# Balancing the gate's sums: one operation folded, six expert items between column sums, a lower rate beside the recurrence

## The chip, the core and the metric

The kernel runs on one core of a Trainium2 chip. The metric is the device time of one launch in microseconds (us). The engines are TensorE (PE; PEld is its loading of weights), VectorE (DVE), ScalarE (ACT), GpSimd (POOL) and SyncE (SP), which issues most transfers.

## What is computed

Three layers, one behind the other. The first is a delta-rule recurrence over 768 steps for 4 x 8 heads of 48; its output is 3072 tokens of 384 channels. The second is a mixture of eight experts in which every token goes through every expert, weighted by a gate matrix P of 3072 x 8 that is balanced by eight rounds of row and column normalization:

```python
    logits = x @ w_gate
    logits = logits - logits.max()
    P = np.exp(logits)
    for _ in range(8):
        P /= P.sum(1, keepdims=True) + 1e-09
        P /= P.sum(0, keepdims=True) + 1e-09
        P *= N / E
    ...
    for e in range(E):
        h = np.maximum(x @ w1[e], 0.0)
        out += P[:, e:e + 1] * (h @ w2[e])
```

The third layer is a feed-forward block with a sigmoid gate (384 to 2048 to 384). Everything is float32; the large products run as three matmuls of split halves each (lines 480 to 482).

## The kernel before

**Recurrence and expert 0 (to about 507 us).** The recurrence is cut into 24 chain steps `u` with four products each: `ks` (L354), `up` (L365), `sp` (L376), `y` (L389). Each needs DVE or ACT between one and the next: L356 makes `r` for `up`, L382 the new state. Every four chain steps share a preparation `prep(g)`: masked products (L181), then the solving of triangular systems on DVE, thirty pairs of L276 and L280, then a transpose (L298) and small products on PE (L307, L316). The steps of `prep` are spread over slots by the table `PIECES`.

To keep PE busy, the work of expert 0, which needs the tokens but not the gate, is cut into 480 **items** of three matmuls each: `g1` (first layer, tile `ph`, 256 columns, three items for one h) and `g2` (second layer, tile `po`, 384 columns). Each h costs one ACT (L626) and one DVE instruction (L627). `slot(t)` puts a number of items into each of the chain's slots: `rate * ITEMS[t % 16]`, where `rate = RATE * 8 / sum(ITEMS)`. So RATE is the mean number of items of two slots; it is 9.6. The first items come at slot LAG.

**Balancing the gate (507 to about 543 us).** After the last logits (transposed by L612 and copied to P by L613) the generator `sinkhorn()` runs while the left-over items go out: every SKN-th item of the loop at L890 advances it by one step. Its steps are: the maximum (L660; L663, a transpose; L665; L668, the matmul that spreads it), subtracting it (L670, L671), the exponential on ACT (L672, with a table load), and eight iterations. One iteration: row sums (L677 to L680, DVE), the sum over a partition's rows (L681), the matmul with ones that sums over partitions (L684, tile `psk`), and then the column scale (L685 to L688). Between two steps stand SKN items, here 5. The same loop issues the loads of the main loop's tokens (`load_x`) at every third item and steps the first main weights (`weights1(0)`, on ACT and POOL) at every third.

**Main loop (from about 543 us).** Seven experts and the third layer, in units of 15 products (`c`) and 12 groups (`po`), with PE as the bound. Tile order, buffers and the program order of all engines are written out by hand (`manual_schedule`).

What sets the order around the change is therefore the code's own order: each engine runs its instructions in the order in which the code emits them, and waits only for data and buffers.

Of the kernel before, what the change touches and what calls it, by code (L numbers as in the profile page):

```python
# [14 lines left out]
ALU = mybir.AluOpType  # L15
# [9 lines left out]
NE = 8  # L25
NT = 3072
# [6 lines left out]


LAG = 10
RATE = 9.6
BURST = 6
SKN = 5


class Attention:
# [400 lines left out]
def kernel(  # L442
# [4 lines left out]
    nc = tc.nc  # L447
# [207 lines left out]
    def sinkhorn():  # L655
        def col(ps_shape):
            return sm["ps"].tile(ps_shape, F32, tag=sm["tag"], name="psk")

        mx = pp.tile([128, 1], F32, name="mx")
        nc.vector.tensor_reduce(out=mx, in_=P.rearrange("p u e -> p (u e)"), op=ALU.max, axis=AX.X)  # L660
        yield
        pt = col([1, 128])
        nc.tensor.transpose(pt, mx, ident)  # L663
        m1 = pp.tile([1, 1], F32, name="m1")
        nc.vector.tensor_reduce(out=m1, in_=pt, op=ALU.max, axis=AX.X)  # L665
        yield
        pb = col([128, 1])
        nc.tensor.matmul(pb, ones[0:1, :], m1, start=True, stop=True)  # L668
        nm = pp.tile([128, 1], F32, name="nm")
        nc.vector.tensor_scalar(out=nm, in0=pb, scalar1=-1.0, scalar2=None, op0=ALU.mult)  # L670
        nc.vector.tensor_scalar(out=P, in0=P, scalar1=nm, scalar2=None, op0=ALU.add)  # L671
        nc.scalar.activation(out=P, in_=P, func=ACTF.Exp)  # L672
        rs = pp.tile([128, NU], F32, name="rs")
        c1 = pp.tile([128, NE], F32, name="c1")
        c2 = pp.tile([128, NE], F32, name="c2")
        for _ in range(8):
            nc.vector.reduce_sum(out=rs, in_=P, axis=AX.X)  # L677
            nc.vector.tensor_scalar(out=rs, in0=rs, scalar1=1e-9, scalar2=None, op0=ALU.add)
            nc.vector.reciprocal(out=rs, in_=rs)
            nc.vector.tensor_tensor(out=P, in0=P, in1=rs.unsqueeze(2).to_broadcast([128, NU, NE]), op=ALU.mult)  # L680
            nc.vector.reduce_sum(out=c1, in_=P.rearrange("p u e -> p e u"), axis=AX.X)  # L681
            yield
            pc = col([128, NE])
            nc.tensor.matmul(pc, ones, c1, start=True, stop=True)  # L684
            nc.vector.tensor_scalar(out=c2, in0=pc, scalar1=1e-9, scalar2=None, op0=ALU.add)  # L685
            nc.vector.reciprocal(out=c2, in_=c2)
            nc.vector.tensor_scalar(out=c2, in0=c2, scalar1=float(NT // NE), scalar2=None, op0=ALU.mult)
            nc.vector.tensor_tensor(out=P, in0=P, in1=c2.unsqueeze(1).to_broadcast([128, NU, NE]), op=ALU.mult)  # L688

    ex = []  # L690
# [1 line left out]
    def expert_item():  # L692
        while ex:
            if next(ex[0], None) is not None:
                return True
            ex.pop(0)
        return False
# [7 lines left out]

    rate = RATE * 8 / sum(ITEMS)
    done, due = 0, 0.0
# [60 lines left out]
    pc = ctx.enter_context(tc.tile_pool(name="pc", bufs=1, space=PSUM, **tw))  # L768
# [117 lines left out]
    loads = [r for r, *_ in SCHEME]  # L886
    w0 = weights1(0)
    sk = sinkhorn()
    sm["ps"], sm["tag"] = pc, "c"
    for i in range(60 * 8 - done):  # L890
        expert_item()
        if i % SKN == 0:
            next(sk, None)
# [274 lines left out]
```

## Time and profile before

| | us |
|---|---|
| three timed runs | 2259.91, 2262.90, 2262.99 (median 2262.9) |
| profiled execution: span from first to last instruction | 2254.7 |
| PE busy in it | 2151.8 (95%) |
| DVE busy | 1525.3 (68%) |
| POOL busy | 1113.1 (49%) |
| ACT busy | 1059.9 (47%) |

The profiled execution's own time is not listed apart from its span; the median of the timed runs is 8.2 us above the span. The shares are averages over stages with different limits. In the first 60 us PE is mostly idle and the recurrence starts alone. From there to 507 us recurrence and expert 0 run side by side, and 507 to 543 us is the balancing of the gate. The rest, three quarters of the time, is the main loop.

### The profile page before, as it was taken

Reading aid. Unit: us, or ns where it says so; the run is one execution under the profiler, and the core shown is the slowest. Engines: PE = TensorE matmul, PEld = TensorE weight load, DVE = VectorE, ACT = ScalarE, POOL = GpSimd, SP = SyncE. Lnnn points to the kernel's source line nnn. Section 1 sums busy time; section 2 is a strip of 40 time slices with the busy share of each in tenths; the row PEclk is TensorE's granted clock in tenths of the full one; section 3 lists DMA queues with packets and bytes.
Section 4 is the critical chain, followed back from the end, with each engine's and each line's share of the span. In section 5 each row is a group of like instructions: output and inputs, shape, how many; then the busy total and the mean of one; then the engine's idle time right before and its main releaser. Section 6 shows DMA issues by size and latency. Waiting matters only on the chain.

```text
span 2254.7 us, 40816 instructions
## 1 busy us (share of the span) xinstructions
PE 2151.8 (95%) x15663; PEld 1935.9 (86%) x15663; DVE 1525.3 (68%) x2770; ACT 1059.9 (47%) x2125; POOL 1113.1 (49%) x1293
## 2 busy tenths in 40 slices
PE   4499999998999999999999999999999999999999
PEld 4388888896989899999998888888989998888888
DVE  6666866626776776666666777777775556676675
ACT  2334343544444444444445444454544446565554
POOL 5521132214677766666552556566665434662333
PEclk7599999999999999999999999999999999999999
DMA  5223333338435343333447655555564465567231
GB/s 116 67 82 83 89 98 101 92 110 312 145 114 182 123 167 134 125 132 114 153 183 252 189 170 183 171 194 175 187 198 143 130 242 170 164 186 240 92 119 50
DMA packets 229155, 336.75 MB, mean 149 GB/s; under 512 B 15648, under 2 KB 192416, under 8 KB 224800
## 3 DMA queue, kind: packets, MB, share of 16 engines
q1 hardware_dynamic: 228240, 333.26, 46.0%
q8 instruction: 123, 2.02, 0.4%
q10 hardware_dynamic: 720, 0.89, 0.1%
q14 instruction: 72, 0.59, 0.1%
HBM read 204.58 MB, written 129.50 MB: 148 GB/s over the span
## 4 chain that ended last, share of the span: by engine, by line
PE 76%; DVE 12%; POOL 3%; DMA 3%; issue 2%; ACT 2%; SPq 1%; POOLq 0%; ACTq 0%; DVEq 0%
PE po L480 13%; PE po L482 13%; PE po L481 13%; PE c L480 10%; PE c L481 9%; PE c L482 9%; DVE ln L280 3%; DVE lt L276 3%; PE pg L181 2%; PE ph L480 1%; DMA w1r<-in_w_dram 1%; POOL w1c L477 1%; PE ph L481 1%; PE ph L482 1%; PE y L389 1%
## 5 line engine op out<-in xcount | busy, mean ns | idle before, releaser
L481 PE MATMUL po<-w2c,h 128*128 128x384 f32 x1728 | 586.8, 340 | 0.0
L482 PE MATMUL po<-w2c,h 128*128 128x384 f32 x1728 | 585.2, 339 | 0.9 <-DVE h L981 0.7
L480 PE MATMUL po<-w2c,h 128*128 128x384 f32 x1728 | 578.4, 335 | 1.0 <-ACT h L979 1.0
L1036 POOL TENSOR_TENSOR acc<-acc,ye 128x384 f32<-128x384 f32 x252 | 264.1, 1048 | 387.1 <-ACT ye L1035 374.0
L480 PE MATMUL c<-xt,w1c 128*128 128x512 f32 x1080 | 430.6, 399 | 11.5 <-DVE h L972 5.5
L482 PE MATMUL c<-xt,w1c 128*128 128x512 f32 x1080 | 429.3, 397 | 1.7 <-POOL w1c L477 1.7
L481 PE MATMUL c<-xt,w1c 128*128 128x512 f32 x1080 | 428.3, 397 | 0.0
L1013 DVE TENSOR_TENSOR o<-o,c 128x512 f32<-128x512 f32 x288 | 197.2, 685 | 251.2 <-PE c L482 232.6
L480 PEld LDWEIGHTS po<-w2c,h 128*128 128x128 f32 x1728 | 324.6, 188 | 40.8 <-ACT h L979 1.6
L481 PEld LDWEIGHTS po<-w2c,h 128*128 128x128 f32 x1728 | 323.5, 187 | 40.0
L1038 DVE SCALAR_TENSOR_TENSOR acc<-po,P,acc 128x384 f32<-128x384 f32 x420 | 257.9, 614 | 147.1 <-PE po L482 143.5
L482 PEld LDWEIGHTS po<-w2c,h 128*128 128x128 f32 x1728 | 324.7, 188 | 1.5 <-DVE h L981 1.5
L1035 ACT ACTIVATE ye<-po,P 128x384 f32<-128x384 f32 x252 | 146.3, 581 | 361.8 <-PE po L482 352.7
L482 PEld LDWEIGHTS c<-xt,w1c 128*128 128x128 f32 x1080 | 202.6, 188 | 47.1 <-POOL w1c L477 2.7
L480 PEld LDWEIGHTS c<-xt,w1c 128*128 128x128 f32 x1080 | 203.0, 188 | 42.7 <-DVE h L972 18.1
L481 PEld LDWEIGHTS c<-xt,w1c 128*128 128x128 f32 x1080 | 203.2, 188 | 9.0
L1006 ACT COPY o<-c 128x512 f32<-128x512 f32 x288 | 163.8, 590 | 54.2 <-PE c L482 53.0
L970 ACT ACTIVATE h<-c 128x512 fp32r<-128x512 f32 x168 | 96.8, 598 | 181.2 <-DVE c L1013 173.4
L1048 POOL TENSOR_TENSOR acc<-acc,ye 128x384 f32<-128x384 f32 x84 | 92.8, 1104 | 166.2 <-ACT ye L1047 156.4
L477 POOL TENSOR_TENSOR w2c<-w2r,w2c 128x384 fp32r<-128x384 f32 x140 | 147.4, 1053 | 45.6 <-ACT w2c L476 45.5
L1013 DVE TENSOR_TENSOR f<-o,c 128x512 f32<-128x512 f32 x216 | 148.9, 689 | 12.4 <-PE c L482 3.4
L970 ACT ACTIVATE h<-f 128x512 fp32r<-128x512 f32 x168 | 100.1, 596 | 79.6 <-DVE f L1013 76.0
(174 smaller groups left out, 3524.5 us busy)
## 6 DMA issues: line engine op xcount, KB each, us to landing
w1c<-wd SPq DMA_DIRECT2D x210, 384.0 KB, 4.5
wd<-w1c SPq DMA_DIRECT2D x28, 1920.0 KB, 7.0
xs<-bo SPq DMA_DIRECT2D x184, 128.0 KB, 2.2
xt<-xs SPq DMA_DIRECT2D x46, 512.0 KB, 5.8
w2r<-in_w_dram SPq DMA_DIRECT2D x55, 384.0 KB, 5.8
wd<-wo SPq DMA_DIRECT2D x56, 256.0 KB, 3.0
w1r<-in_w_dram SPq DMA_DIRECT2D x28, 384.0 KB, 7.6
x<-in_kq_dram SPq DMA_DIRECT2D x24, 384.0 KB, 6.6
```

The source lines that it names most:

```text
L276: nc.vector.tensor_tensor(out=t3, in0=ln[:, jj + 1:32, jj:jj + 1].to_broadcast([128, nr, jj]), in1=ln[:, jj:jj + 1, 0:jj].to_broadcast([12 ...
L477: eng.tensor_tensor(out=dst_lo, in0=src, in1=dst_hi.bitcast(F32), op=ALU.subtract)
L480: nc.tensor.matmul(ps, lhs[0], rhs[0], start=start, stop=False, **kw)
L481: nc.tensor.matmul(ps, lhs[0], rhs[1], start=False, stop=False, **kw)
L482: nc.tensor.matmul(ps, lhs[1], rhs[0], start=False, stop=stop, **kw)
L970: nc.scalar.activation(out=h[:, 0], in_=src, func=ACTF.Relu)
L1006: nc.scalar.copy(out=o, in_=ps)
L1013: nc.vector.tensor_tensor(out=d, in0=o, in1=ps, op=ALU.add if how == "add" else ALU.subtract)
L1035: nc.scalar.mul(ye, ps, P[:, u, e:e + 1])
L1036: nc.gpsimd.tensor_tensor(out=a, in0=a, in1=ye, op=ALU.add)
L1038: nc.vector.scalar_tensor_tensor(out=a, in0=ps, scalar=P[:, u, e:e + 1], in1=a, op0=ALU.mult, op1=ALU.add)
L1048: nc.gpsimd.tensor_tensor(out=a, in0=a, in1=ye, op=ALU.add)
```

## The change

Three constants and one operation. RATE goes from 9.6 to 9.2, so each slot of the recurrence gets 4% fewer items, and more are left for the loop behind it. SKN goes from 5 to 6. In the column scale, the factor NE / NT is multiplied in by the second operation of the instruction that adds 1e-9, ahead of the reciprocal, instead of NT / NE by an instruction of its own behind it.

```diff
-RATE = 9.6
+RATE = 9.2
 BURST = 6
-SKN = 5
+SKN = 6
...
             pc = col([128, NE])
             nc.tensor.matmul(pc, ones, c1, start=True, stop=True)
-            nc.vector.tensor_scalar(out=c2, in0=pc, scalar1=1e-9, scalar2=None, op0=ALU.add)
+            nc.vector.tensor_scalar(out=c2, in0=pc, scalar1=1e-9, scalar2=float(NE) / NT, op0=ALU.add, op1=ALU.mult)
             nc.vector.reciprocal(out=c2, in_=c2)
-            nc.vector.tensor_scalar(out=c2, in0=c2, scalar1=float(NT // NE), scalar2=None, op0=ALU.mult)
             nc.vector.tensor_tensor(out=P, in0=P, in1=c2.unsqueeze(1).to_broadcast([128, NU, NE]), op=ALU.mult)
```

Behind this place, line numbers of the changed kernel are one lower.

On PE, in the recurrence (rows with + are the changed kernel's, with - the kernel's before; `ph` and `po` are items of expert 0, `w1s` and `w2s` its weights):

```order
 L482 MATMUL po<-w2s_196,h 128x384
+L354 MATMUL ks<-S,x_126 64x48 x16
 L480 MATMUL ph<-xb,w1s_191 128x256
 L481 MATMUL ph<-xb,w1s_191 128x256
 L482 MATMUL ph<-xb,w1s_191 128x256
-L354 MATMUL ks<-S,x_126 64x48 x16
```

The chain's product comes one item earlier; such differences add up to 17 items at the last logits.

On DVE, one iteration of the balancing before (`psk` is the sum over partitions, `c_6935` the column scale):

```order
L685 TENSOR_SCALAR c_6935<-psk 128x8
L686 RECIPROCAL c_6935<-c_6935 128x8
L687 TENSOR_SCALAR c_6935<-c_6935 128x8
L688 TENSOR_TENSOR P<-P,c_6935 128x192
L677 TENSOR_REDUCE rs<-P 128x24
L678 TENSOR_SCALAR rs<-rs 128x24
L679 RECIPROCAL rs<-rs 128x24
L680 TENSOR_TENSOR P<-P,rs 128x192
L681 TENSOR_REDUCE c_6934<-P 128x8
L627 SCALAR_TENSOR_TENSOR h<-ph,h 128x256
```

And one after, with the same names:

```order
L685 TENSOR_SCALAR c_6877<-psk 128x8
L686 RECIPROCAL c_6877<-c_6877 128x8
L687 TENSOR_TENSOR P<-P,c_6877 128x192
L677 TENSOR_REDUCE rs<-P 128x24
L678 TENSOR_SCALAR rs<-rs 128x24
L679 RECIPROCAL rs<-rs 128x24
L680 TENSOR_TENSOR P<-P,rs 128x192
L681 TENSOR_REDUCE c_6876<-P 128x8
L627 SCALAR_TENSOR_TENSOR h<-ph,h 128x256
```

The scalar instruction between reciprocal and product is gone, and the order of the others is kept.

On ACT, around the exponential before (`ye` is a result of expert 0 that is written out, `lg` the logits, `w1c` the first main weights):

```order
L606 COPY lg<-pl 8x256
L626 ACTIVATE h<-ph 128x256 x2
L642 COPY ye<-po 128x384
L643 DMA yd<-ye 128x384
L642 COPY ye<-po 128x384
L643 DMA yd<-ye 128x384
L672 ACT_TABLE_LOAD
L672 ACTIVATE P<-P 128x192
L626 ACTIVATE h<-ph 128x256 x3
L476 CAST w1c<-w1r 128x256
```

And after:

```order
L606 COPY lg<-pl 8x256
L626 ACTIVATE h<-ph 128x256 x3
L672 ACT_TABLE_LOAD
L672 ACTIVATE P<-P 128x192
L626 ACTIVATE h<-ph 128x256
L476 CAST w1c<-w1r 128x256
L626 ACTIVATE h<-ph 128x256
L476 CAST w1c<-w1r 128x128
L642 COPY ye<-po 128x384
L643 DMA yd<-ye 128x384
```

The two results `ye` that stood ahead of the table load stand behind the exponential.

## Rows read from the trace of the kernel before

**Rows 1.** Windows, 180 to 507 us: length, PE, PEld, DVE, ACT, POOL busy, PEclk, DMA.

```profile
180.00:209.00 29.00, 27.02 (x377) 24.59 (x375) 27.63 (x81) 9.97 (x25) 3.76 (x4) 1.00 0.41 111
209.00:252.00 43.00, 43.00 (x772) 37.15 (x768) 22.22 (x49) 19.01 (x36) 9.04 (x7) 1.00 0.29 76
252.00:283.00 31.00, 28.89 (x415) 25.90 (x416) 29.10 (x88) 11.40 (x28) 4.09 (x4) 1.00 0.40 103
...
322.00:358.00 36.00, 33.12 (x421) 30.45 (x418) 33.51 (x89) 13.59 (x33) 10.37 (x14) 0.91 0.44 111
...
400.00:433.00 33.00, 30.49 (x429) 28.03 (x427) 30.87 (x80) 13.36 (x32) 6.25 (x11) 1.00 0.35 104
433.00:507.00 74.00, 74.00 (x1143) 68.16 (x1135) 18.71 (x39) 34.07 (x76) 15.88 (x27) 1.00 0.31 93
```

**Rows 2.** Timeline of PE in the recurrence: start, duration, instruction, [idle before <- releaser].

```profile
337.41 1.94 PE L365 MATMUL up<-r,tt 64*64 64x48 f32 x32 [2.31 <-DVE r L356]
...
414.79 1.13 PE L365 MATMUL up<-r,tt 64*64 64x48 f32 x32 [1.49 <-DVE r L356]
```

**Rows 3.** Timeline of PE from the last logits to the main loop.

```profile
507.11 0.28 PE L612 MATMUL pt<-ident,lg 8*128 8x8 f32 x2
...
512.90 0.38 PE L668 MATMUL psk<-m,ones 1*128 1x1 f32 x2
...
517.85 0.39 PE L684 MATMUL psk<-c,ones 128*128 128x8 f32 x2 [2.59 <-DVE c L681]
...
539.27 0.39 PE L684 MATMUL psk<-c,ones 128*128 128x8 f32 x2 [0.74 <-DVE c L681]
...
542.63 0.39 PE L684 MATMUL psk<-c,ones 128*128 128x8 f32 x2 [0.23 <-DVE c L681]
542.88 0.48 PE L480 MATMUL c<-xt,w1c 128*128 128x512 f32 x1
```

**Rows 4.** Timeline of DVE in one iteration of the balancing.

```profile
536.79 0.17 DVE L687 TENSOR_SCALAR c<-c 128x8 f32<-128x8 f32 x1
537.00 0.36 DVE L688 TENSOR_TENSOR P<-P,c 128x192 f32<-128x192 f32 x1
...
539.13 0.42 DVE L627 SCALAR_TENSOR_TENSOR h<-ph,h 128x256 fp32r<-128x256 f32 x1
```

**Rows 5.** Timelines of DVE and ACT around the exponential.

```profile
513.51 0.62 DVE L671 TENSOR_SCALAR P<-P,nm 128x192 f32<-128x192 f32 x1
...
514.28 1.28 ACT L672 ACT_TABLE_LOAD   x1 [0.39 <-ACT ye L642]
515.58 0.36 ACT L672 ACTIVATE P<-P 128x192 f32<-128x192 f32 x1
```

**Rows 6.** Timeline of PE: two matmuls of a first-layer and of a second-layer item.

```profile
537.13 0.28 PE L480 MATMUL ph<-xb,w1s 128*128 128x256 f32 x1
537.25 0.28 PE L481 MATMUL ph<-xb,w1s 128*128 128x256 f32 x1
...
541.37 0.33 PE L481 MATMUL po<-w2s,h 128*128 128x384 f32 x1
541.54 0.33 PE L482 MATMUL po<-w2s,h 128*128 128x384 f32 x1
```

**Rows 7.** Timelines of DVE and POOL at two long DVE instructions.

```profile
526.00 0.71 DVE L687 TENSOR_SCALAR c<-c 128x8 f32<-128x8 f32 x1
...
524.86 1.82 POOL L477 TENSOR_TENSOR w1c<-w1v,w1c 128x768 fp32r<-128x768 f32 x1 [2.06 <-ACT w1c L476]
...
543.87 0.86 DVE L688 TENSOR_TENSOR P<-P,c 128x192 f32<-128x192 f32 x1
...
543.76 0.75 POOL L834 TENSOR_TENSOR w1v<-w1r 128x256 f32<-128x256 f32 x1
```

**Rows 8.** Windows behind two waits of PE, columns as in rows 1 (PEclk third from last).

```profile
337.40:343.90 6.50, 6.49 (x49) 6.41 (x50) 5.58 (x15) 2.19 (x5) 0.00 (x0) 0.50 0.02 6
414.80:418.00 3.20, 3.20 (x47) 3.10 (x47) 2.96 (x9) 1.43 (x3) 0.00 (x0) 1.00 0.00 0
```

## The prediction

> **What bounds the kernel now.** I read the windows of busy time first, to see which engine limits which stretch, then the timeline around the column sums, where most of TensorE's (PE's) idle time after the start lies. Behind 545 us PE is nearly always busy and the change leaves the order of work there as it is, so the question is how long PE takes to reach that point. PE's work in front of it is the same before and after: 480 expert items and the recurrence. Only PE's idle time can change.
>
> Beside the recurrence two engines take turns. In four stretches (180 to 209, 252 to 283, 322 to 358, 400 to 433 us) VectorE (DVE) solves the triangular systems: it is busy for 27.6 of 29.0 us in the first, in some 80 instructions, and the gaps are the hand-overs between them. PE stands idle for 1.98, 2.11, 2.88 and 2.51 us in these, 9.5 us in all, though it is nearly full too. Between them PE has no gap: 43.00 of 43.00 us, and at the end 74.00 of 74.00 [rows 1]. Where PE does wait, it is for what DVE makes late, as the product with r in the third and the fourth solve, 2.31 and 1.49 us [rows 2].
>
> Behind the recurrence come the alternating sums (the tail): from the transpose of the last logits, 507.11 us, to the first product of the main loop, 542.88, it is 35.77 us [rows 3]. The DVE chain sets the pace: the eighth sum's matmul starts 3.36 us behind the seventh's, although PE has only five items to do in between. An item is three matmuls with a start-to-start of 0.12 us (first layer) or 0.17 us (second) [rows 6], so 0.36 or 0.51 us. In 480 items first and second stand 24 to 16, which makes 0.42 us on average. Five items are some 2.1 us in a period of 3.36. And in front of the first of the eight sums PE waits 2.59 us [rows 3]. The 51 items of this tail are worth 27 x 0.36 + 24 x 0.51 = 22.0 us of its 35.77.
>
> **What moves.** Counting items in the program's order: at the transpose of the last logits 429 items lie behind PE before, 412 after; 17 items go from beside the recurrence into the tail, which has 68 instead of 51. Two of the 17 are gone by the product with r of chain step 5, 15 leave between there and the end. Between two sums there are six items instead of five, and behind the eighth sum seven (one first, six second) instead of none. The eight iterations lose one DVE instruction each.
>
> **Recurrence.** If PE were the bound everywhere, 17 x 0.42 = 7.1 us would go. In the four solves it isn't: they are 29 + 31 + 36 + 33 = 129 of the 357 us from 150 to 507, 36% [rows 1]. I put 36% of the 15 items, 5.4, into them. There an item is worth only its share of DVE: one instruction of 0.42 us (L627 [rows 4]) in five items, 5.4 x 0.42 / 5 = 0.45 us. The other 9.6 items are worth 9.6 x 0.42 = 4.0 us. The two early ones I give nothing (in full they would be 0.8). Sum: the recurrence ends **4.5 us** earlier. The bounds: 7.1 us from above; from below, if only the two windows in which PE never waited [rows 1] give all of it back, 117 / 357 x 15 x 0.42 = 2.1 us. The cover that hides an item's removal in a solve is DVE's own queue; if that cover is thinner than I think, the gain goes up, not down.
>
> **Tail, up to the first sum.** From the last logits (T0) to the matmul that spreads the maximum (L668) it is now 5.79 us for 11 items [rows 3], which by their kinds are 3 x 0.36 + 8 x 0.51 = 5.2, so 0.6 us of small matmuls. After it is 13 items, 8 first and 5 second: 5.4 + 0.6 = 6.0. From L668 to the first sum it is 4.95 us now [rows 3]. Of this, the exponential waits: its input was ready at 513.51 + 0.62 = 514.13, but the table load began only at 514.28 and the exponential at 515.58 [rows 5], because two evictions of an expert's result stood ahead of the load on ScalarE (ACT). In the new order these two stand behind the exponential, and what stands ahead is an eviction of h, done by about L668. The load then runs beside L670 and L671 and the exponential can start near 514.17, 1.4 us earlier by this clock. That gives 4.95 - 1.4 = 3.55, and the first sum at T0 + 9.6 us instead of 10.74. PE's six items there (2.6 us) are hidden.
>
> A page speaks against this. The Trainium skill, "ScalarE: Activation LUTs", section "What ACT_TABLE_LOAD costs", counts a switch at about 2.66 us, 1.28 for the load and the rest for a drain. The trace doesn't agree here: the exponential starts at 515.58, 0.02 us behind the end of a load of 1.28 us [rows 5]. By the page's price the exponential would come 1.4 us later than I take it and the result would be 2260.7 us.
>
> **Tail, the eight sums.** Removed are eight L687, 0.17 us and 0.04 us to the next instruction [rows 4], so the period of 3.36 becomes 3.15 us; six items are 2.6 us and the sum's matmul 0.25 [rows 3], so DVE still sets it, with PE close behind. Seven periods: 22.05 us. With six items one period gets two L627, and in another the h comes out of the last item before the sum, so its L627 stands late in DVE's queue ahead of the next sum's first instruction; I take 0.4 us for each, 0.8 together. Between nothing and these 0.8 I choose the upper value, since the order shows both.
>
> Some L687 took longer: 0.71 us at 526.00, ending with GpSimd's (POOL's) subtraction of 524.86 + 1.82. It reads as a wait of 0.54 us for POOL. The removal would give this back if the next instruction were free of it. But L688, with both inputs in SBUF, took 0.86 us instead of 0.36 at 543.87, beside POOL's work of 543.76 [rows 4, 7]. So the wait passes on to the next instruction, and I count it as kept: 0.5 us, half of the 0.54 + 0.50 seen, from zero to 1.0, because other instructions meet POOL's now. The Trainium skill, "SBUF — State Buffer", section "Who interferes with whom", says the same against this part of the change: a DVE instruction with two SBUF inputs also blocks against a GpSimd instruction that reads SBUF. Without that rule the forecast would be 0.5 us lower.
>
> Behind the eighth sum: 0.25 us for its matmul and 0.36 + 6 x 0.51 = 3.4 of items, with 0.1 for the hand-over: 3.75 us, where it was 0.25. Sum of the tail: 9.6 + 22.05 + 0.8 + 0.5 + 3.75 = 36.7 us, **0.9 us longer** than now, with 17 items more in it. The lower bound is 9.6 + 22.05 + 3.75 = 35.4 (0.4 shorter); the upper has the exponential no earlier (1.4) and all of the POOL waits (another 0.5): 38.6, 2.8 longer.
>
> Folding the scale into the addition itself costs nothing: L685 stays one instruction on the same eight columns. The transfers for the main loop are issued at the same item numbers of a longer tail, so they land earlier against its start; I count nothing for it.
>
> **Sum.** 4.5 - 0.9 = 3.6 us less. The profiled span of 2254.7 becomes 2251.1. The median of the three runs lies 8.2 us above that span, and I leave this distance: **2259.3 us**. The bounds together: gain of 7.1 + 0.4 = 7.5 (2255.4) to 2.1 - 2.8 = -0.7 (2263.6).
>
> **Rivals.**
> (a) PE is the bound beside the recurrence after all: DVE's lateness in the solves comes from PE's own lateness, and the full 7.1 us come off. Then 2262.9 - 7.1 + 0.9 = 2256.7. For it: PE is 92 to 93% busy even in the solves. Against: DVE is busy for 93 to 95% of each of them [rows 1], and PE waits for its results there [rows 2].
> (b) Slower: PE's waits grow until the clock falls. Behind the wait of 2.31 us the granted clock was 0.50, the lower of its two levels (1.2 and 2.4 GHz), for 337.40 to 343.90; behind that of 1.49 us it stayed at 1.00 [rows 2, 8]. Fewer items leave about 0.57 us more waiting in each solve (5.4 x 0.42 / 4). That would bring the 1.49 to 2.1, and if it and its like in the two other solves reached 2.3, each would cost half of 6.5 us: 3 x 3.25 = 9.75, to 2269.0. It decides from 2.3 us on in one wait; against it, the additions fall 0.2 us short at the worst place and more elsewhere.
> (c) The change moves work but frees nothing: only the windows without a wait give time back (2.1) and the tail takes its upper bound (2.8 longer): 2263.6.
>
> **How the numbers follow.** The forecast has 50% (2257 to 2261.5), (a) 28%, (c) 14%, (b) 8%. A measurement of this kernel can tell about 0.2%, 4.5 us, from no change. Faster than that means below 2258.4: all of (a) and some 8 of the forecast's 50, 36%. Slower means above 2267.4: (b), 8%. The rest, 56%, lies within. The range from 2256.0 to 2264.0 takes in the forecast, (a) and (c), and leaves out (b) and the outer ends.
>
> **What would show it.** The time of the last logits' transpose: 502.6 us if the recurrence is as I say, near 500 for (a). From there to the main loop's first product: 36.7. In front of the first sum PE should wait under 1 us instead of 2.59, and the half clock behind it should be gone. Period of the sums: near 3.2. The half clock near 337 us should neither vanish nor have companions. I am wrong if the main loop, from its first product to the end, changes by more than 2 us: then something is moved that I did not see.

## The result: slower, and outside the range

The changed kernel takes 2288.2 us (median of six runs, 2271.9 to 2295.6) against 2263.0 for the kernel before in the same comparison: a ratio of 1.0095, 95% interval 1.007 to 1.012. Forecast were 2259.3 us and a range of 2256.0 to 2264.0. The profiled execution is one of the quicker ones: 2274.9 us, span 2273.2. Of its 18.5 us more than the profile before, 9.8 lie in front of the last logits, 5.3 in the tail and 3.4 in the main loop.

TensorE (PE) in the tail after, to be read against [rows 3] (start, duration, instruction, [idle before <- releaser]):

```profile
516.90 0.28 PE L612 MATMUL pt<-ident,lg 8*128 8x8 f32 x2
...
522.94 0.38 PE L668 MATMUL psk<-m,ones 1*128 1x1 f32 x2
...
526.77 0.39 PE L684 MATMUL psk<-c,ones 128*128 128x8 f32 x2 [0.61 <-DVE c L681]
...
533.12 0.39 PE L684 MATMUL psk<-c,ones 128*128 128x8 f32 x2
...
539.07 0.60 PE L684 MATMUL psk<-c,ones 128*128 128x8 f32 x2 [2.09 <-DVE c L681]
...
544.46 0.43 PE L684 MATMUL psk<-c,ones 128*128 128x8 f32 x2
...
550.84 0.39 PE L684 MATMUL psk<-c,ones 128*128 128x8 f32 x2 [0.21 <-DVE c L681]
```

The last logits (T0) come at 516.90 instead of 507.11; 502.6 was forecast. From there to the main loop's first product (557.96) it is 41.06 us instead of 35.77. The first sum is where it should be, 9.87 us behind T0, with 0.61 us of waiting. But the fourth and the fifth sum come 5.95 and 5.39 us behind the one before them, where 3.15 was forecast.

PE's waits beside the recurrence, to be read against [rows 2]. `issue` means that PE waited for nothing that the profile names:

```profile
296.59 0.65 PE L181 MATMUL pg<-x 48*64 48x128 f32 x6 [0.30 <-issue]
...
340.02 1.27 PE L365 MATMUL up<-r,tt 64*64 64x48 f32 x19 [2.98 <-DVE r L356]
...
376.00 0.87 PE L181 MATMUL pg<-x 48*64 48x128 f32 x12 [1.07 <-issue]
...
411.43 0.42 PE L480 MATMUL ph<-xb,w1s 128*128 128x256 f32 x1 [2.75 <-DVE h L627]
...
485.78 1.52 PE L365 MATMUL up<-r,tt 64*64 64x48 f32 x24 [5.36 <-ACT h L626]
```

The wait of 2.31 us has become 2.98, and there are new ones: two with no visible cause, one of 2.75, and one of 5.36 us, the largest between 150 us and T0. Windows with the granted clock (third from last), to be read against [rows 1, 8]:

```profile
209.00:252.00 43.00, 42.75 (x770) 37.17 (x771) 22.17 (x51) 19.00 (x36) 9.42 (x8) 1.00 0.29 76
...
336.00:347.00 11.00, 7.76 (x64) 7.19 (x65) 9.77 (x26) 2.19 (x5) 0.19 (x1) 0.53 0.06 17
...
433.00:517.00 84.00, 77.75 (x1185) 72.31 (x1183) 22.89 (x47) 37.07 (x82) 19.26 (x34) 0.96 0.29 86
...
483.00:491.00 8.00, 5.22 (x47) 5.01 (x47) 1.78 (x4) 3.64 (x9) 5.37 (x10) 0.57 0.00 0
```

The last stretch in front of T0, in which PE had no gap before (74.00 of 74.00 us), has 6.25 us of idle time now, and near 340 and 487 us the clock is at its lower level. The two stretches between solves that carried the forecast's gain give nothing back: from `up` of step 7 to that of step 9 it is 43.8 us instead of 44.0, and from `up` of step 19 to T0 83.0 instead of 77.3.

### The profile page after: what moved, and what is told of

It is laid out like the page before. It is cut to its first block, busy times and chain, and to the rows that moved or that the text cites. A ratio compares the mean times of both kernels' runs of the same rounds, so it can differ in the third digit from the quotient of the medians.

```text
span 2273.2 us, 40799 instructions
## 1 busy us (share of the span) xinstructions
PE 2159.6 (95%) x15663; PEld 1945.3 (86%) x15663; DVE 1526.8 (67%) x2762; ACT 1059.6 (47%) x2125; POOL 1113.2 (49%) x1293
## 3 DMA queue, kind: packets, MB, share of 16 engines
q8 instruction: 123, 2.02, 0.3%
## 4 chain that ended last, share of the span: by engine, by line
PE 76%; DVE 12%; POOL 3%; DMA 3%; ACT 2%; issue 2%; SPq 1%; POOLq 0%; ACTq 0%; DVEq 0%
PE po L482 13%; PE po L480 13%; PE po L481 13%; PE c L480 10%; PE c L481 9%; PE c L482 9%; DVE ln L280 3%; DVE lt L276 3%; PE pg L181 2%; PE ph L480 1%; DMA w1r<-in_w_dram 1%; POOL w1c L477 1%; PE ph L481 1%; PE ph L482 1%; PE up L365 1%
## 5 line engine op out<-in xcount | busy, mean ns | idle before, releaser
L1034 ACT ACTIVATE ye<-po,P 128x384 f32<-128x384 f32 x252 | 146.3, 581 | 359.4 <-PE po L482 346.3
```

The lines of the kernel that those rows point to most:

```text
L1034: nc.scalar.mul(ye, ps, P[:, u, e:e + 1])
```

## The experiments

All 18 experiments in one table, below the two kernels; what each is for follows. Ratio: to the kernel before in the same comparison. T0 and the stalls (`issue`, over 0.2 us) are from the profiled execution, and "half clock" is the time at 0.50 between 150 us and T0, worked out from windows of 1 us.

| kernel | median | ratio, 95% | T0 | half clock | stalls |
|---|---|---|---|---|---|
| before | 2263.0 | | 507.1 | 6.8 | none |
| after | 2288.2 | 1.0095 (1.007 to 1.012) | 516.9 | 20.4 | 0.30, 1.07 |
| e1 RATE alone | 2294.4 | 1.0138 (1.0113 to 1.0162) | 534.6 | 54.6 | 2.05, 2.23 |
| e2 all but RATE | 2265.7 | 1.0008 (0.9993 to 1.0023) | 508.2 | 6.8 | none |
| e3 no lump | 2282.7 | 1.0086 (1.0052 to 1.0121) | 531.5 | 54.6 | 2.64, 2.04 |
| e4 writes on ScalarE's queue | 2301.3 | 1.0163 (1.0131 to 1.0195) | 545.5 | 75.0 | 1.81, 1.91 |
| e5 after, one block | 2288.1 | 1.0107 (1.0075 to 1.0138) | 528.0 | 40.9 | 2.20, 0.25 |
| e6 after, two blocks | 2294.3 | 1.0125 (1.009 to 1.0159) | 543.3 | 68.1 | 1.92, 1.68 |
| e7 before, one block | 2266.8 | 1.0012 (0.9997 to 1.0027) | 512.6 | 13.6 | none |
| e8 no lump, one block | 2281.0 | 1.0073 (1.0045 to 1.0102) | 519.2 | 30.7 | 1.92 |
| e9 after, half a block | 2274.0 | 1.0050 (1.0028 to 1.0072) | 517.9 | 27.2 | none |
| e10 before, half a block | 2266.8 | 1.0020 (0.9998 to 1.0041) | 517.2 | 20.5 | 1.15 |
| e11 no lump, half a block | 2268.1 | 1.0022 (1.0007 to 1.0037) | 516.5 | 23.8 | none |
| e12 x later | 2274.3 | 1.0051 (1.0032 to 1.0069) | 517.5 | 27.2 | none |
| e13 as e11, RATE 8.8 | 2265.8 | 1.0017 (1.0005 to 1.0029) | 506.0 | 20.4 | none |
| e14 before, RATE 10.0 | 2307.0 | 1.0196 (1.0173 to 1.0218) | 557.0 | 64.8 | none |
| e15 fold alone | 2262.0 | 0.9996 (0.9985 to 1.0008) | 511.0 | 13.6 | none |
| e16 before, fillers | 2265.9 | 1.0012 (0.9998 to 1.0026) | 510.6 | 6.8 | none |
| e17 e11, fillers | 2267.9 | 1.0018 (1.0004 to 1.0033) | 512.9 | 10.2 | 1.41 |
| e18 e13, fillers | 2268.7 | 1.0027 (1.0011 to 1.0042) | 502.6 | 6.8 | none |

### Which part of the change: e1 to e4

My first theory came from the two programs' order, read once more. Tokens arrive in batches of 40 items, one every two chain steps, and the loop at L737 (`while u % 2 == 1 and len(ex) > 1`) must finish a batch before the next is split, since `xb` has two buffers. RATE 9.6 just keeps up. RATE 9.2 falls behind, and the rest is done in one piece, a **lump**, between `up` and the transposes of x: 3, 7, 10 and 13 items at chain steps 17, 19, 21 and 23. I had counted items at T0, 17 fewer, and taken them as evenly spread.

The kernel before with the new rate alone (e1):

```diff
-RATE = 9.6
+RATE = 9.2
```

> The kernel before with one number changed: RATE 9.2 in place of 9.6. In its order 3, 7, 10 and 13 expert items stand in one piece ahead of the transposes of x at chain steps 17, 19, 21 and 23. If these lumps make the kernel slower (theory L): last logits after 512 us, median 2272 to 2295 us. If the fold or the sixth item between two sums does it (theory F): last logits near 503, median 2258 to 2264.

The changed kernel with the old rate (e2):

```diff
-RATE = 9.2
+RATE = 9.6
```

> The changed kernel with RATE back at 9.6: fold and six items stay, no lumps. Theory L: last logits near 507 us, median 2258 to 2266. Theory F: median 2272 or more.

The changed kernel with three buffers under the tag `xb` and one under `x32` (e3):

```diff
-                while u % 2 == 1 and len(ex) > 1:
+                while u % 2 == 1 and len(ex) > 2:
```

> The changed kernel with a third buffer for x, and one batch of items allowed to stay over: the same 412 items before the last logits, but spread evenly, with no lump. Theory L: the even spread gives the gain that I predicted, last logits near 503 us, median 2255 to 2262. Rival Q, a late result write at the head of SyncE's queue holds up the loads for the sums: part of the loss stays, median 2266 or more, and POOL's sums still stand beside DVE's solve. Rival C, with fewer items the chain of the recurrence is simply exposed: last logits 515 or later, median 2272 to 2295.

The changed kernel with all result writes on ScalarE's queue (e4):

```diff
-                    (nc.sync if n < 10 else nc.scalar).dma_start(out=yd[2 * n + k], in_=ye)
+                    nc.scalar.dma_start(out=yd[2 * n + k], in_=ye)
```

> The changed kernel with the expert results of the recurrence written by ScalarE's queue in place of SyncE's, so that no write stands ahead of the loads for the sums; the lumps stay. Theory L: as the changed kernel, median 2272 to 2295, the waits at steps 21 to 23 stay. Rival Q: the load for the sums at step 22 is issued some 4 us earlier, GpSimd and the solve wait less, median 2262 to 2268.

RATE is the whole loss (e1, e2); the fold and the sixth item together cost nothing that can be measured. Rival Q falls: with the writes off SyncE's queue it is slower still, above the range of theory L too, and from step 21 to 23 it takes 36.4 us, no less than the changed kernel's 34.6. But e3 misses too: without a lump 2282.7 us remain, as rival C had it; e11 and e13 come back to C. The start of `up` tells where the time goes:

| start of `up` at chain step | 11 | 12 | 15 | 16 | 21 | 23 | T0 |
|---|---|---|---|---|---|---|---|
| before | 279.6 | 301.9 | 355.4 | 380.0 | 464.2 | 492.4 | 507.1 |
| after | 279.7 | 302.8 | 358.0 | 382.8 | 467.8 | 502.4 | 516.9 |
| e1 | 279.5 | 309.8 | 367.0 | 398.5 | 484.5 | 520.1 | 534.6 |
| e3 | 282.4 | 313.3 | 370.4 | 401.7 | 489.6 | 517.1 | 531.5 |
| e9 | 279.8 | 303.6 | 357.8 | 382.0 | 468.7 | 503.4 | 517.9 |
| e11 | 281.1 | 304.9 | 359.4 | 388.0 | 473.1 | 502.0 | 516.5 |
| e13 | 281.4 | 302.6 | 354.3 | 381.4 | 464.4 | 491.7 | 506.0 |

The lump is real where it is largest: from step 21 to 23 after and e1 need 34.6 and 35.6 us, e3 27.5, the kernel before 28.2. The lump puts off x: its copy to memory is issued 3.7 us behind the start of `up` of step 21 in the kernel before (first row), 7.8 us behind it in the changed kernel (second row):

```profile
467.90 0.51 SPq L525 DMA_DIRECT2D xf<-x  x1
...
475.62 0.52 SPq L525 DMA_DIRECT2D xf<-x  x1
```

The load of the sums (`braw`) stands behind that copy, and GpSimd (POOL) waits for it. Behind POOL's first additions (L549) stand its scaling of v (L112), which r on DVE needs, and on ScalarE (ACT) a copy of the sums (L555), behind which ACT's h (L626) comes late. Rows of the changed kernel on ACT, POOL and DVE:

```profile
483.65 0.40 ACT L555 CAST bo<-bv 128x256 fp32r<-128x256 f32 x1 [6.16 <-POOL bv L549]
...
481.93 0.86 POOL L549 TENSOR_TENSOR bv<-braw 128x128 f32<-128x128 f32 x2 [20.53 <-DMA braw<-xf]
...
483.57 1.47 POOL L112 TENSOR_TENSOR v<-v,nn 128x768 f32<-128x768 f32 x1
...
485.08 0.56 DVE L356 TENSOR_TENSOR r<-ks,v 128x384 f32<-128x384 f32 x1 [7.13 <-POOL v L112]
```

The product `up` needs r, which is done at 485.64, and starts at 485.78: that is where the 5.36 us of PE's wait come from. But e1 and e3 lose 8 to 9 us at step 12 as well and 7 at step 16, where no lump is.

### Instruction blocks that come late: e5 to e12

PE in e1 between steps 11 and 12, and windows behind it (columns as above):

```profile
296.70 0.86 PE L181 MATMUL pg<-x 48*64 48x128 f32 x10
299.62 0.65 PE L181 MATMUL pg<-x 48*64 48x128 f32 x6 [2.05 <-issue]
300.74 1.88 PE L181 MATMUL pg<-x 48*64 48x128 f32 x16
...
300.00:314.00 14.00, 14.00 (x107) 11.29 (x106) 7.94 (x23) 2.02 (x5) 2.26 (x3) 0.53 0.00 1
...
386.00:404.00 18.00, 17.74 (x131) 14.41 (x131) 8.44 (x24) 2.39 (x6) 3.60 (x6) 0.53 0.01 2
```

PE stops in the middle of sixteen equal matmuls for 2.05 us, and behind that the clock stays at its lower level for nearly 14 us. The second stall, at 386, is followed by 17. Each costs, as an estimate, 2 us and half of what follows, some 9 to 11 us; the steps there are 8.0 and 6.9 us longer than before. The transfers of e1 from 293 to 297 us and in the microsecond behind (queue, kind: packets, MB, share of 16 engines), with SyncE's issue of x ahead of them:

```profile
291.49 0.33 SPq L102 DMA_DIRECT2D x<-in_kq_dram  x1
...
q1 hardware_dynamic: 155, 0.66, 82.9%
...
q8 instruction: 1, 0.02, 7.4%
q1 hardware_dynamic: 5, 0.00, 0.6%
```

q8 is the queue that brings PE's instructions: over the whole run it moves 123 packets with 2.02 MB, for 15,663 matmuls and as many weight loads, so some 255 instructions in a packet of 16 KB. The Trainium skill, "Runtime: NRT & Kernel Launch", section "Instruction fetch mechanics", gives such blocks of 256 instructions and calls their cost mostly hidden. The size agrees; that it is hidden doesn't hold here, where the stalls of the table reach 2.64 us. Count PE's matmuls and weight loads in blocks of 256, and number the packets from 0: packet k usually moves when the count has reached k plus 0.3 to 0.8. At these two places of after, e1 and e3 it moves at k plus 1.1 to 1.5. In e1 the block of 284 us is followed by none until 297, when the transfer of x (768 KB, 292.4 to 297.3) is nearly over. Over all twenty traces, from 150 us to T0, the fifteen stalls of the table each stand within 4 us behind a block that moved at 1.1 or later; all twelve blocks that moved at 1.4 or later have a stall of 1.15 us or more behind them, and those that moved before 1.1 have none.

So theory I: with 9.2 the items shift PE's instructions, and now a block falls due beside a transfer of x. A rival, N, says that the place of the code is nothing. Matmuls that nobody reads, put ahead of everything on PE, move the block ends and nothing else. The edit as in e5, e7 and e8; e6 has 64 calls in each of the two tiles, and e9 to e11 have 16:

```diff
+    for _ in range(2):
+        pad = psg.tile([32, 8], F32, tag="g", name="pad")
+        for _ in range(32):
+            nc.tensor.matmul(pad, ones[0:64, 0:32], ones[0:64, 0:8], start=True, stop=True)
     prep = chain.from_iterable(A.prep(g) for g in range(NG))
```

> The changed kernel with 64 tiny matmuls ahead of everything on TensorE, whose results nobody reads: with their weight loads 128 instructions, half of one 16 KB block of TensorE's instruction queue, so that the blocks end half a block earlier in the program. Nothing else moves. Theory I (an instruction block that falls due beside a transfer of x comes late, PE stalls near 296 and 376 us and the granted clock falls behind it): the stalls named issue near 296 and 376 us vanish or shrink under 0.3 us, the steps up to 300 us start as in the kernel before, median 2262 to 2275. Rival N (the code's place is nothing, the loss is the late items alone): median stays at 2285 to 2296 and the stalls stay.

> The changed kernel with 128 such tiny matmuls ahead, 256 instructions, one whole block: the blocks end at the same places of the program as in the changed kernel. Theory I: the stalls near 296 and 376 us are as in the changed kernel, median 2275 to 2296, above the half block's. If the tiny matmuls help by something else (a warmer clock, a later start), it is at or below the half block's time.

> The kernel before with the same 64 tiny matmuls ahead. Theory I: now a block falls due near 292 us, just ahead of the transfer of x at 292.5, and one near 369.5 inside that of 367 to 372: stalls of 0.3 to 2.5 us named issue appear, each with up to 7 us of half clock, median 2265 to 2285. Rival N: 2260 to 2266, no stall.

> The third x buffer (items spread evenly, no lump) and the half block together in the changed kernel. If the instruction blocks and the lumps are all there is: last logits near 507 us, median 2258 to 2266. If the predicted gain of an even spread were real beside that: last logits near 503, median 2254 to 2260. If fewer items expose the chain by themselves: median 2270 or more.

None of the four moved. The trace says why: I had counted one matmul for a call, and it is two, so that these were shifts of one and two whole blocks:

```profile
1.58 7.00 PE L701 MATMUL pad<-ones 64*32 64x8 f32 x128 [1.58 <-POOL ones L454]
```

They are controls: after stays slow (e5, e6), before stays as it was (e7), e8 is like e3, and the stall is in the same sixteen matmuls. Then half a block (e9 to e11), and in e12 the other side of the meeting, the transfer, in the changed kernel:

```diff
+            if s == 3 and u % 2 == 0 and 4 <= u // 2 + 3 < 12:
+                A.load_x(u // 2 + 3)
...
             A.load_k(u // 2 + 4)
-            A.load_x(u // 2 + 4)
```

In e12 the load stands behind some masked products that need it, so these take the x of an earlier group; the instructions and their sizes are the same.

> The trace of the kernels with 64 tiny calls showed 128 matmuls and one more instruction block, so that those shifts were one and two whole blocks. Here are 32 calls, 64 matmuls with 64 weight loads, half a block, in the changed kernel. Theory I (instruction block beside a transfer of x): the issue stall near 296 us goes or moves to another matmul, as does that near 376; step 12 starts within 1.5 us of the kernel before's 301.9; median 2262 to 2282. Rival N (the stall belongs to the place in the program, not to the block): stalls and median as before, 2282 to 2296.

> The kernel before with the same half block ahead. Theory I: a block now falls due near 292 us, just ahead of the transfer of x, and one near 369.5 inside another: stalls named issue of 0.3 to 2.5 us appear, each with some half clock, median 2266 to 2285. Rival N: no stall, median 2260 to 2267.

> Changed kernel, third x buffer and half a block together: no lump, and no block late. If these two are all of the loss, median 2256 to 2266, last logits at or before 508 us. If fewer items also expose the chain, 2268 or more.

> The changed kernel with the loads of x issued three pieces of a chain step later; TensorE's instructions are the same, only the transfer moves by some 10 to 18 us. Theory I: no issue stall near 296 and 376 us unless the moved transfer meets another block; step 12 starts within 1.5 us of 301.9; median 2262 to 2282. If the stall is not from the transfer: it stays, 2282 to 2296.

Theory I holds. With half a block, and with the same code but x moved, the stalls are gone, step 12 is back at 303.6 and 302.9, and the medians are 14 us lower, 2274.0 and 2274.3 (10 us by the ratios, 1.0095 to 1.0050). In e9 the sixteen matmuls run through, and the clock stays up where e1 had its lower level:

```profile
297.00 1.09 PE L181 MATMUL pg<-x 48*64 48x128 f32 x16
...
300.00:314.00 14.00, 14.00 (x187) 11.50 (x187) 9.75 (x29) 3.66 (x9) 4.92 (x4) 1.00 0.34 101
```

One limit: the profiled execution of the changed kernel itself is a quick one, with stalls of only 0.30 and 1.07 us, step 12 at 302.8 and T0 no later than e9's. That its slower executions have the long stalls is read from e5 and e6, the same kernel shifted by whole blocks (stalls of up to 2.20 and 1.92 us, T0 528.0 and 543.3); no trace of such an execution of its own is at hand.

And half a block gives the kernel before a stall that it did not have, though not where I expected it: beside the transfer of x issued at 218.86, one group of chain steps earlier.

```profile
226.91 1.65 PE L181 MATMUL pg<-x 48*64 48x128 f32 x13 [1.15 <-issue]
...
226.00:245.00 19.00, 18.09 (x131) 14.43 (x131) 8.40 (x24) 2.88 (x7) 4.16 (x4) 0.55 0.01 2
```

Steps 9 to 14 start 10 us later in that execution. The median is only 2.9 us above the kernel before's, which its interval (0.9998 to 1.0041) doesn't tell from nothing, and the timed runs reach from 2259.6 to 2277.3; presumably the two don't meet in every run, which was not tried. What stays open is how the transfer holds a block back. One block of the kernel before moved at 295.00, in the middle of such a transfer (291.4 to 297.0), at 0.64 by the count, so hardly late; one at 223.60 moved at 1.07, only when its transfer was over, with no stall behind it.

With the lumps gone too (e11) it is 2268.1 us: 6 us less than e9, as the 34.7 us from step 21 to 23 (e9) become 28.9; the intervals of the two ratios still overlap. What is left is 0.22% (0.07 to 0.37), just inside the range that I had given for a chain exposed by fewer items.

### What an item beside the recurrence is worth: e13, e14, e16 to e18

No kernel with RATE 9.2 reaches T0 earlier than the kernel before, and at step 11 none is ahead by more than 0.6 us, although seven items are gone by then. Either each chain step takes as long as its own chain (C), or the items are worth their time (P) and something takes it back.

Kernel e11 with fewer items still (e13):

```diff
-RATE = 9.2
+RATE = 8.8
```

> The kernel with the third x buffer and half a block ahead (no lump, no block late), with RATE 8.8 in place of 9.2: 17 items fewer again before the last logits, 10 of them before step 13. If each chain step is as long as its own chain (theory C): step 13 and the last logits start where they did with 9.2 (324 and 516 us, within 2), the tail takes the items at 0.42 us each, median 2272 to 2282. If items are worth their time on TensorE (theory P, the prediction's): step 13 4 us earlier, last logits 7 us earlier, median 2264 to 2270. A block that falls due beside a transfer of x would show as an issue stall.

The kernel before with more (e14):

```diff
-RATE = 9.6
+RATE = 10.0
```

> The kernel before with RATE 10.0 in place of 9.6: 18 items more before the last logits, 8 of them before step 13. Theory C: step 13 starts within 1 us of 321.6, and the last sums run with no items beside them, median 2255 to 2264. Theory P: step 13 at 325, last logits at 514, median 2260 to 2268. An issue stall is possible, since the blocks move.

And fillers ahead of `up`, in the kernel before (e16), in e11 (e17) and in e13 (e18):

```diff
+        for _ in range({6: 1, 10: 1, 14: 2, 18: 2}.get(u, 0)):
+            nc.tensor.matmul(up.rearrange("p h d -> p (h d)"), self.ident,
+                             self.ident.unsqueeze(1).to_broadcast([128, 3, 128]), start=True, stop=True)
```

> The kernel before with one (chain steps 6 and 10) or two (14 and 18) matmuls of 128x384 on the identity ahead of the product up, whose result up overwrites. They run while TensorE waits for r. If the waits pull the clock down: no half clock near 337 us, last logits up to 3.4 us earlier, median 2258 to 2263. If it falls for another reason: half clock stays at 6.8 us up to the last logits, and the extra work makes it 0 to 3 us slower.

> The same fillers in the changed kernel with the third x buffer and half a block ahead (no lump, no late block; 2268.1 us without them, 23.8 us of half clock before the last logits). If the waits pull the clock down: half clock near 192, 285 and 339 us goes, last logits 5 us earlier, near 511, median 2260 to 2266. If not: 2267 to 2272.

> The same fillers with RATE 8.8 (2265.8 us without them, 20.4 us of half clock before the last logits at 506). If the waits pull the clock down: last logits near 501, median 2258 to 2263, at or under the kernel before. If not: 2265 to 2270.

C alone falls with e13: all its ten runs (2265.1 to 2271.3 us) stay below the 2272 that C asks for, and 17 items fewer than in e11 bring T0 10.5 us earlier, more than their 7.1 us; 3.4 us less of half clock are 1.7 of it. But 34 items fewer than the kernel before, 14 us of PE's work, bring it 1.1 us (2.5 without the pads' 1.4), and the tail grows from 35.8 to 47.2 us. RATE 10.0 does worse than both theories allow: items run out of tokens, PE waits for `xb` (1.85 us at 157.6, 1.86 at 242.3), and T0 is 50 us later. 9.6 stands between two edges: above it the batch is not there yet, below it lumps form.

The fillers (0.81 us, or 1.45 for two) do what they were for in the profile: no half clock near 338 us in e16 (though 6.8 us of it near 356 instead), and 10.2 and 6.8 us in all before T0 instead of 23.8 and 20.4 in e17 and e18. Yet the medians do not follow: 2267.9 and 2268.7 against 2268.1 and 2265.8 without. So the clock behind these waits is not shown to be what took the gain. Single profiled executions differ by several us in T0, as much as is looked for here (e15 below has the kernel before's program up to T0, and 511.0 instead of 507.1), and where the last 0.2% went beside the recurrence **stays open**.

### The fold alone: e15

```diff
-            nc.vector.tensor_scalar(out=c2, in0=pc, scalar1=1e-9, scalar2=None, op0=ALU.add)
+            nc.vector.tensor_scalar(out=c2, in0=pc, scalar1=1e-9, scalar2=float(NE) / NT, op0=ALU.add, op1=ALU.mult)
             nc.vector.reciprocal(out=c2, in_=c2)
-            nc.vector.tensor_scalar(out=c2, in0=c2, scalar1=float(NT // NE), scalar2=None, op0=ALU.mult)
```

> The kernel before with the scale folded into the addition and nothing else. The prediction counted 0.21 us for each of the eight sums: tail 1.7 us shorter, from the last logits to the first product of the main loop 34.1 in place of 35.8, median 0.5 to 2.5 us under the kernel before's. If TensorE's five items set the period, nothing.

No difference can be measured, and the tail of the profiled execution is 39.4 us, not 34.1. DVE and POOL there:

```profile
530.05 2.04 DVE L687 TENSOR_TENSOR P<-P,c 128x192 f32<-128x192 f32 x1
...
532.51 1.80 DVE L678 TENSOR_SCALAR rs<-rs 128x24 f32<-128x24 f32 x1
...
530.03 1.84 POOL L477 TENSOR_TENSOR w1c<-w1v,w1c 128x768 fp32r<-128x768 f32 x1 [3.01 <-ACT w1c L476]
532.49 1.80 POOL L477 TENSOR_TENSOR w1c<-w1v,w1c 128x768 fp32r<-128x768 f32 x1 [0.61 <-ACT w1c L476]
```

Two DVE instructions of 0.36 and 0.18 us take 2.04 and 1.80: each starts 0.02 us behind a subtraction of POOL and ends 0.2 us behind it or with it. The iteration takes 6.45 us. These two meetings alone cost 3.3 us, more than the 1.7 us that the fold removes in eight iterations; whether the fold brings them about or this execution's timing does was not tried. The Trainium skill, "SBUF — State Buffer", section "Who interferes with whom", has such contention for a DVE instruction with two SBUF inputs, and says that a `tensor_scalar` can have it too; the rows agree.

## Why the prediction was wrong, point by point

- **The step that failed is "Recurrence"**: 4.5 us earlier, bounds 2.1 to 7.1. T0 was 9.8 us later in the profiled execution. The term priced the items that leave and took their places as even. It did not look at where the others then stand (the lump, 6 us of the median, e9 to e11) nor at what else the shift moves, PE's instruction blocks against the transfers of x (10 to 14 us, after to e9 and e12). Neither was among the rivals. The lump stood in the order of the two programs; the blocks could not be seen there, only as a queue on the profile's page. With both taken away (e11), T0 is 516.5 in its trace and the lower bound of 2.1 us is not seen either; why an even spread gives nothing back stays open.
- **Rival (b)** had the right kind of loss, waits that end in half clock, at 2269.0. The wait of 2.31 grew to 2.98, as it said in kind, but what pulled the clock down most in e1 and e3 were the two stalls, which it did not have. Its bar of 2.3 us in one wait does not hold either: behind the stall of 1.15 us in e10 the clock was at its lower level for 17 us, and behind that of 1.07 us in the changed kernel it stayed up.
- **Tail up to the first sum**: right. 9.87 us for 9.6, PE's wait 0.61 for "under 1", and the half clock behind it is gone (granted clock 0.72 from 518 to 524 us before, 1.00 from 527 to 532 after). The exponential starts 0.02 us behind the end of its table load again:

```profile
522.93 1.28 ACT L672 ACT_TABLE_LOAD   x1
524.23 0.36 ACT L672 ACTIVATE P<-P 128x192 f32<-128x192 f32 x1
```

- **Tail, the eight sums**: the term of 0.8 us for late L627 was mis-sized: the seven periods take 27.4 us where 23.35 was forecast, 0.8 and 0.5 for POOL's waits included. The undisturbed period is 3.17 to 3.31 us, near the 3.15 forecast. In the fourth, L627 stands in DVE's queue ahead of the sum's first instruction and waits 2.09 us for its h, which ACT makes late: two results `ye` and two casts of 0.83 us stand ahead of it there. Behind that L687 meets POOL, 1.23 us instead of 0.36.

```profile
534.01 0.83 ACT L476 CAST w1c<-w1v 128x768 fp32r<-128x768 f32 x1 [0.40 <-ACT ye L642]
534.75 0.65 ACT L626 ACTIVATE h<-ph 128x256 fp32r<-128x256 f32 x2
...
535.15 0.42 DVE L627 SCALAR_TENSOR_TENSOR h<-ph,h 128x256 fp32r<-128x256 f32 x1 [2.09 <-ACT h L626]
...
535.92 1.23 DVE L687 TENSOR_TENSOR P<-P,c 128x192 f32<-128x192 f32 x1
```

  Then comes half clock, 0.57 from 537 to 545 us, and the fifth period is 5.39. So the two results that I was glad to see move from ahead of the table load to behind it came back two periods later: 41.06 us for 36.7.
- **Main loop**: 3.4 us longer where I allowed 2. Over the kernels whose sums all end ahead of it this stretch varies from 1709 to 1716 us, so the bound was too narrow to tell anything.
- **Sum**: the profiled execution before was among the quickest of its kernel. Its time is its span and some 1.7 us, 2256.4, and the 8.2 us that I added were spread between executions.

## What to carry to other kernels

A change in how many work items fill a stretch also moves the rest of the program on every queue: read the new order for pieces that a buffer limit forces together, not only the count at the end. And shift the program by half an instruction block before a loss of some us is put down to the change itself: here that was about half of it, with no instruction of the computation touched.

## What was not expected of the hardware

PE ran out of instructions, so an engine does not wait for data and buffers alone, as the section on the kernel before has it. A block of 16 KB that fell due as a transfer of 768 KB began came some 4 us late (due near 292.8 us by PE's count, moved at 297.0 in e1), PE stood for 1.8 to 2.6 us at that place in e1, e3, e4, e5, e6 and e8, and the clock was at its lower level for some 14 us behind it. And a matmul call on plain float32 tiles, such as those ahead of everything in e5, is two matmuls in the trace, with two weight loads (64 calls gave 128), so the blocks pass twice as fast there as a count of calls says.
